# Transposing by halves of 64 rows in a gated-linear-attention and mixer kernel, and copying the first transposes out in two pieces

## The chip, the cores and the metric

The kernel runs on one core of one Trainium2 chip. The metric is device time in microseconds (us) of one execution. Three runs of the kernel before gave 180.56, 180.7 and 180.9 us; the median is 180.7.

## The reference

Two parts follow one another. The first is a recurrent attention with a decaying state, for 4 batches, 8 heads, 768 steps and 48 numbers a head:

```python
for t in range(S):
    state = alpha[:, :, t, :, None] * state + np.einsum('bhd,bhe->bhde', k[:, :, t], v[:, :, t])
    y[:, :, t] = np.einsum('bhd,bhde->bhe', q[:, :, t], state)
```

Its result, laid out as 4 x 768 x 384, goes through a mixer with a residual:

```python
xt = x.transpose(0, 2, 1)
h = np.maximum(xt @ w_tok1, 0.0) @ w_tok2          # 768 -> 256 -> 768, along the steps
u = x + h.transpose(0, 2, 1)
h2 = np.maximum(u @ w_ch1, 0.0) @ w_ch2            # 384 -> 1536 -> 384, along the channels
return (u + h2).astype(np.float32)
```

## The kernel before, in words

**Attention.** Each batch has 6 chunks of 128 steps. ScalarE takes the logarithm of alpha (`la`, L360), TensorE sums it along the chunk with a triangular matrix (`cum`, L461, or L531 and L533), ScalarE makes the exponentials of that sum (`ek` L373, `eq` L375), and GpSimd or VectorE multiplies keys and queries by them (`pkk`, `pkq`, L392). Both products lie with steps on the 128 partitions. TensorE transposes them (L409 or L557): the data is the loaded operand, an identity is the one that streams, and the result lies in a bank of PSUM. ScalarE or VectorE copies that to SBUF (`tk`, `tq`, L413 or L563). From the transposes TensorE makes the scores within a chunk (`gt`, L477 or L574), VectorE masks them (`gm`, L418), and TensorE multiplies them by the values (`y`, L510 or L607), to which it adds the earlier chunks' share (`between`, L447). The state goes through L498 or L595 on TensorE, then `st` and `ss` (L428, L431, L435). The result `x` is copied out at L442.

**Two forms of a chunk.** In batches 0 and 1 (`PLAN` has P there) chunks come in pairs, `paired_chunks`: row p of the two halves of a load holds steps 2p and 2p+1, and rows 0 to 63 belong to the one chunk, 64 to 127 to the other. Some of its matmuls therefore use 64 rows and run in two row halves in turn (L595, L607), or in 64x64 quarters (L574). A pair has 16 transposes, 8 of keys and 8 of queries, in two banks. Batches 2 and 3 (N) use `natural_chunk`: 8 transposes a chunk, 4 and 4, in two banks; its L477 uses 48 of 64 rows in two halves in turn.

**Mixer.** `mixer(b)` has `tok1` (L655, for batch 0 in parts at L635), `tok2` (L674), the residual `u` (L682, L685), the transposes of `u` (L698, 18 of 128x128 a batch) and their copies `ut` (L704), `ch1` (L723, 72 matmuls a batch), its relu `rt` (L642, L644), `ch2` (L738, 72 matmuls a batch) and the sum and the store of the output (L747, L749). In batch 0 the copies of `ut` come in two halves of 3 chunks, in batches 1 to 3 as one piece of 768 columns for each of the 3 blocks of channels.

**Order.** No engine's order is written by hand. Every step is an `Op` in a `Graph`, with a cost for each engine that may run it and a priority that places batch b+1's attention ahead of batch b's `ch1` and `ch2`. `run` simulates the engines: whenever one is free it takes the ready step of best priority, if enough of the 8 banks of PSUM are free. Up to 32 us of that simulation an idle TensorE gets a dummy matmul (L795, 78 in all). `search` tries 600 random changes of the priorities and engines of batch 0, by the simulated end of its `ut` copies. The order found is then emitted, and on the chip every engine works through its own list in order, waiting where an operand is late. A changed cost can so move any step of any engine. Within the simulation a step that writes a bank waits for all earlier readers of that bank.

Of the kernel before, what the change touches and what calls it, by code (L numbers as in the profile page):

```python
# [200 lines left out]
def kernel(  # L201
# [83 lines left out]
    tk_t = many("tk", NG, [128, 4, 128])  # L285
    tq_t = many("tq", NG, [128, 4, 128])
# [7 lines left out]
    ut_t = many("ut", 2 * NM, [128, S])  # L294
# [106 lines left out]
    def s_transpose(n, w, dst, key, prio):  # L401

        u, bank = units[n], Bank()
        src, ksrc = u["p" + w]

        def emit(e):
            ps = banks[bank.place].bitcast(BF16)
            for j in range(4):
                pe.transpose(ps[:, 128 * j : 128 * j + 128], src[:, 2 * j : 2 * j + 2, :], id128)  # L409

        g.add("tr" + w, {"PE": 0.225}, emit, [ksrc], [bank], prio, new=[bank])
        g.add("tp" + w, {"ACT": 0.52, "DVE": 0.40},
              lambda e: evict[e](dst, banks[bank.place].bitcast(BF16)[:, 0:512].rearrange("p (j t) -> p j t", j=4)),  # L413
              [bank], [key], prio)
# [36 lines left out]
    def natural_chunk(n):  # L451
# [17 lines left out]
        tk, tq, i = tk_t[n % NG], tq_t[n % NG], n % NG  # L469
        s_transpose(n, "k", tk, ("tk", i), pr + 2)  # L470
        s_transpose(n, "q", tq, ("tq", i), pr + 2)
        gb = [Bank(), Bank()]

        def gt(e):
            for j in range(4):
                for par in range(2):
                    pe.matmul(banks[gb[par].place][:, 128 * j : 128 * j + 128],  # L477
                              lhsT=tk[64 * par : 64 * par + D, j, :],
                              rhs=tq[64 * par : 64 * par + D, j, :], start=True, stop=True,
                              skip_group_check=True)  # L480

        g.add("gt", {"PE": 0.24}, gt, [("tk", i), ("tq", i)], gb, pr + 1, new=gb)
# [24 lines left out]
        def y(e):  # L507
# [4 lines left out]
            if ci:  # L512
                between(ps, tq, n)

        g.add("y", {"PE": 0.37 if ci else 0.21}, y, [("gm", 2 * i), ("gm", 2 * i + 1), kvb, ("tq", i)] + ([kprev] if ci else []),
# [3 lines left out]
    def paired_chunks(b, sc):  # L519
# [28 lines left out]
        ktk, ktq = ("tk2", i2), [("tq2", i2)]  # L548
        for w in "kq":
            bank = Bank()  # L550
            for s in range(2):
                src, ksrc = us[s]["p" + w]

                def emit(e, w=w, s=s, src=src, bank=bank):
                    ps = banks[bank.place].bitcast(BF16)
                    for j in range(4):
# [277 lines left out]
```

## Time and profile before

| | |
|---|---|
| median of 3 runs | 180.7 us |
| the profiled execution | 180.38 us |
| its span, first to last instruction | 178.7 us |
| TensorE matmuls, busy | 172.5 us, 97% |
| ScalarE, VectorE, GpSimd busy | 100.8, 96.4, 69.1 us |
| granted clock of TensorE | 1.00 |

Time outside the span is 1.68 us. The busy time of TensorE is a sum over intervals whose ends are modelled and which overlap: the pace of a stream of matmuls is read from the starts of successive rows of the timeline, not from the length of one. In a timeline row the first number is the start, the second the length of the whole row, then come engine, line, operation, output and inputs, loaded shape (rows x columns), result shape, and the number of instructions; a bracket gives idle time ahead of the row and what ended it.

### The profile page before, as it was taken

The numbers are of one execution on the slowest core, as the hardware profiler recorded it, in microseconds if no ns is written. First come the engines' busy times: TensorE is split into PE (matmuls) and PEld (weight loads), VectorE is DVE, ScalarE is ACT, GpSimd is POOL, SyncE is SP. The second block draws the span as 40 slices with busy tenths as digits, with TensorE's granted clock in tenths as the row PEclk, the third lists the DMA queues.
The fourth block names the chain that finished last, engine by engine and source line by source line (L and its number), as shares of the span: only waits on it lengthen the run. The fifth ranks groups of instructions, "written<-read, shape, count | busy, mean of one in ns | idle before, by whom it ended". The sixth has DMA issues, their size and how long they took to land.

```text
span 178.7 us, 4775 instructions
## 1 busy us (share of the span) xinstructions
PE 172.5 (97%) x1929; PEld 112.4 (63%) x1929; DVE 96.4 (54%) x197; ACT 100.8 (56%) x206; POOL 69.1 (39%) x111
## 2 busy tenths in 40 slices
PE   6999999999999998999999999999999999999991
PEld 2667666666666766677666566676766666565650
DVE  3269895602277967698982632499754362000321
ACT  2586384699765455678776330598872230996000
POOL 7341580000878975929951111398850000000000
PEclk9999999999999999999999999999999999999999
DMA  5999999999999898989999999700000112100222
GB/s 138 261 261 260 237 283 206 203 218 257 271 265 276 191 233 151 247 154 195 158 202 148 205 193 253 219 0 4 0 4 32 55 45 91 44 0 4 88 88 88
DMA packets 81797, 27.83 MB, mean 156 GB/s; under 512 B 75376, under 2 KB 81520, under 8 KB 81776
## 3 DMA queue, kind: packets, MB, share of 16 engines
q1 hardware_dynamic: 79424, 25.17, 65.7%
q0 software_dynamic: 2352, 2.36, 8.3%
q8 instruction: 15, 0.25, 0.6%
q14 instruction: 6, 0.05, 0.1%
HBM read 25.17 MB, written 4.72 MB: 167 GB/s over the span
## 4 chain that ended last, share of the span: by engine, by line
PE 85%; POOL 7%; issue 3%; DVE 2%; POOLq 0%; DVEq 0%
PE bank L723 26%; PE bank L738 21%; PE bank L795 8%; PE bank L674 4%; PE bank L655 3%; PE bank L409 3%; PE bank L698 2%; PE bank L557 2%; POOL pkq L392 2%; PE bank L477 2%; POOL ss L431 2%; POOL pkk L392 2%; PE bank L447 2%; PE bank L510 1%; PE bank L461 1%
## 5 line engine op out<-in xcount | busy, mean ns | idle before, releaser
L723 PE MATMUL bank<-ut,wc 128*128 128x384 bf16 x288 | 51.9, 326 | 0.0
L738 PE MATMUL bank<-wc,rt 128*128 128x384 bf16 x288 | 50.3, 326 | 0.0
L642 ACT ACTIVATE rt<-bank 128x384 bf16<-128x384 f32 x73 | 35.6, 492 | 8.3 <-PE bank L723 7.8
L738 PEld LDWEIGHTS <-rt 128*128 128x128 bf16 x288 | 27.3, 98 | 17.0
L392 POOL TENSOR_TENSOR pkk<-ink,ek 128x384 bf16<-128x384 f32 x24 | 23.8, 998 | 33.0 <-ACT ek L373 30.9
L723 PEld LDWEIGHTS <-wc 128*128 128x128 bf16 x288 | 26.6, 98 | 15.3
L747 DVE TENSOR_TENSOR o<-bank,u 128x384 f32<-128x384 f32 x24 | 13.3, 556 | 36.7 <-PE bank L738 36.6
L399 POOL CAST vb<-inv 128x384 bf16<-128x384 f32 x22 | 10.8, 503 | 25.0 <-DMA inv<-in_v_dram 25.0
L373 ACT ACTIVATE ek<-bank 128x384 f32<-128x384 f32 x24 | 11.8, 501 | 14.5 <-PE bank L464 9.9
L795 PE MATMUL bank<-zeros,id 128*128 128x384 bf16 x78 | 17.0, 354 | 1.8 <-DVE la L300 1.8
L644 DVE TENSOR_SCALAR rt<-bank 128x384 bf16<-128x384 f32 x23 | 12.3, 554 | 11.4 <-PE bank L723 11.1
L360 ACT ACTIVATE la<-ina 128x384 bf16<-128x384 f32 x24 | 12.1, 529 | 10.6 <-DMA ina<-in_alpha_dram 10.5
L392 POOL TENSOR_TENSOR pkq<-inq,eq 128x384 bf16<-128x384 f32 x18 | 18.0, 998 | 0.0
L418 DVE TENSOR_TENSOR gm<-bank,u 128x512 bf16<-128x512 f32 x24 | 15.4, 683 | 1.2 <-PE bank L477 1.2
L418 DVE TENSOR_TENSOR gm<-bank,pmask 128x512 bf16<-128x512 f32 x24 | 15.0, 683 | 1.4 <-PE bank L574 1.0
L685 DVE TENSOR_TENSOR u<-bank,x 128x384 bf16<-128x384 f32 x21 | 10.3, 550 | 5.7 <-PE bank L674 5.7
L795 PEld LDWEIGHTS <-id 128*128 128x128 bf16 x78 | 7.7, 105 | 6.9 <-POOL id masks.py:199 1.8
L431 POOL TENSOR_TENSOR ss<-st,al 128x384 bf16<-128x384 f32 x12 | 9.9, 827 | 4.0 <-DVE st L428 4.0
L442 ACT CAST x<-bank 128x384 bf16<-128x384 f32 x15 | 7.3, 487 | 5.8 <-PE bank L447 3.6
L375 ACT ACTIVATE eq<-bank 128x388 f32<-128x388 f32 (+2 forms) x18 | 9.2, 511 | 0.0
L674 PE MATMUL bank<-ht,wt 128*128 128x384 bf16 x48 | 8.9, 326 | 0.0
L704 ACT COPY ut<-bank 128x768 bf16<-128x768 bf16 (+1 forms) x8 | 5.5, 722 | 5.8 <-PE bank L698 5.8
(95 smaller groups left out, 209.0 us busy)
## 6 DMA issues: line engine op xcount, KB each, us to landing
out_dram<-o SPq DMA_DIRECT2D x24, 192.0 KB, 2.6
ina<-in_alpha_dram SPq DMA_DIRECT2D x6, 384.0 KB, 6.1
ink<-in_k_dram SPq DMA_DIRECT2D x6, 384.0 KB, 6.2
inq<-in_q_dram SPq DMA_DIRECT2D x6, 384.0 KB, 6.5
inv<-in_v_dram SPq DMA_DIRECT2D x6, 384.0 KB, 6.5
ina<-in_alpha_dram SPq DMA_DIRECT2D x12, 192.0 KB, 4.6
ink<-in_k_dram SPq DMA_DIRECT2D x12, 192.0 KB, 4.6
inq<-in_q_dram SPq DMA_DIRECT2D x12, 192.0 KB, 4.5
```

What stands on the lines that cost most here:

```text
L360: g.add("la", {"ACT": 0.43}, lambda e: act.activation(la[:, :, 0:D], t, AF.Ln), key, [u["la"][1]], pr + 5)
L373: g.add("ek", {"ACT": 0.40}, lambda e: act.activation(ek, banks[bank.place][:, 0:HD], AF.Exp, scale=-1.0), [bank], [kek], pr + 4)
L392: lambda e, dst=dst, src=src, ex=ex: {"POOL": gps, "DVE": dve}[e].tensor_tensor(dst[:, :, 0:D], src, ex().rearrange("p (h d) -> p h d", h= ...
L418: g.add("gm", {"DVE": 0.62}, lambda e: dve.tensor_tensor(gm, banks[bank.place].rearrange("p (j t) -> p j t", j=4), wide(mask, [[0, 4], lis ...
L431: g.add("ss", {"POOL": 0.97}, lambda e: gps.tensor_tensor(ss, st.rearrange("p (h d) -> p h d", h=H), wide(al, [[1, 8], [0, D]]), ALU.mult) ...
L642: act.activation(dst, src, AF.Relu)
L644: dve.tensor_scalar_max(dst, src, 0.0)
L674: pe.matmul(banks[bank.place][:, 0:HD], lhsT=wt2[:, m, i * 128 : i * 128 + 128], rhs=ht_t[b % 2 * NDT + m], start=(m == 0 and not on_act), ...
L723: pe.matmul(banks[bank.place][:, 0:HD], lhsT=wc1[wp][:, kc, off : off + 128], rhs=ut_t[(b % 2) * NM + kc][:, cs], start=(kc == 0), stop=(k ...
L738: pe.matmul(banks[bank.place][:, 0:HD], lhsT=rt_t[(b * NDC + mc) % NRT][:, i * 128 : i * 128 + 128], rhs=wc2[:, mc, :], start=(mc == 0), s ...
L747: g.add("o", {"DVE": 0.49}, lambda e, i=i, bank=bank, o=o: dve.tensor_tensor(o, banks[bank.place][:, 0:HD], u_t[(n0 + i) % NX], ALU.add), ...
L795: return Op("fill", {"PE": 0.33 if now < COLD else 0.17}, lambda e: pe.matmul(banks[N_BANKS - 1][:, 0:HD], lhsT=id128, rhs=zeros, start=Tr ...
```

## The change

Batches 1 to 3 no longer transpose a 128x128 block with one matmul. Rows 0 to 63 and rows 64 to 127 are transposed by two matmuls that follow each other, each with 64 rows loaded and 64 columns streaming, and each half goes to a bank of its own. This holds for keys and queries of `paired_chunks` when b is not 0, for `natural_chunk`, and for the transposes of `u`. A chunk's keys and queries then share the two banks, and the copies take a half each. `ut` becomes one tile for all channel blocks and is made in two groups of 3 chunks in every batch; `ch1` of one half of the columns waits for its own group.

In batch 0 the transposes stay whole; keys and queries of a pair are copied out by two copies of 512 columns each where one of 1024 stood, and the scores of one half of the keys wait only for their part. Some costs that the planner uses are changed with it (`gt`, `state`, `y`).

```diff
+    def row_tiles(place, srcs):
+        for i, src in enumerate(srcs):
+            for h in range(2):
+                rows = slice(64 * h, 64 * h + 64)
+                pe.transpose(banks[place[h].place].bitcast(BF16)[:, 64 * i : 64 * i + 64], src[rows], id128[rows, rows])
+
-    def s_transpose(n, w, dst, key, prio):
-        u, bank = units[n], Bank()
...
-        g.add("tr" + w, {"PE": 0.225}, emit, [ksrc], [bank], prio, new=[bank])
-        g.add("tp" + w, {"ACT": 0.52, "DVE": 0.40},
...
+    def s_transpose(n, dst, key, prio):
+        u, tb = units[n], [Bank(), Bank()]
+        srcs = [u["p" + w][0][:, 2 * j : 2 * j + 2, :] for w in "kq" for j in range(4)]
+        g.add("tr", {"PE": 0.28}, lambda e: row_tiles(tb, srcs), [u["pk"][1], u["pq"][1]], tb, prio, new=tb)
+        for h in range(2):
+            g.add("tp", {"ACT": 0.52, "DVE": 0.40}, lambda e, h=h: evict[e](
+                dst.rearrange("p w j t -> p (w j) t")[:, :, 64 * h : 64 * h + 64],
+                banks[tb[h].place].bitcast(BF16)[:, 0:512].rearrange("p (x t) -> p x t", t=64)),
+                [tb[h]], [(*key, h)], prio)
...
-        g.add("gt", {"PE": 0.24}, gt, [("tk", i), ("tq", i)], gb, pr + 1, new=gb)
+        g.add("gt", {"PE": 0.28}, gt, ktkq, gb, pr + 1, new=gb)
...
+        if b == 0:
+            for w in "kq":
+                bank = Bank()
...
+                for part in range(2):
+                    def evicted(e, w=w, bank=bank, part=part):
...
+                    g.add("tp" + w, {"ACT": 0.52, "DVE": 0.40} if w == "k" else {"ACT": 0.52, "DVE": 0.65}, evicted,
+                          [bank], [(ktk if w == "k" else ktq)[part]], pr + 2)
+        else:
+            tb = [Bank(), Bank()]
+            for w in "kq":
+                for s in range(2):
+                    src, ksrc = us[s]["p" + w]
+                    def emit(e, w=w, s=s, src=src):
+                        at = 512 * (w == "q") + 256 * s
+                        for j in range(4):
+                            for c in range(2):
+                                rows = slice(64 * c, 64 * c + 64)
+                                pe.transpose(banks[tb[c].place].bitcast(BF16)[:, at + 64 * j : at + 64 * j + 64],
+                                             src[rows, 2 * j : 2 * j + 2, :], id128[rows, rows])
+                    g.add("tr" + w, {"PE": 0.14}, emit, [ksrc], tb, pr + 2, new=tb if (w, s) == ("k", 0) else [])
+                for c in range(2):
...
+                    g.add("tp" + w, {"ACT": 0.52, "DVE": 0.40} if w == "k" else {"ACT": 0.52, "DVE": 0.65}, evicted,
+                          [tb[c]], [(ktk if w == "k" else ktq)[c]], pr + 2)
...
-            g.add("gt", {"PE": 0.24}, gt, [ktk, *ktq], gb, pr + 1, new=gb)
+            g.add("gt", {"PE": 0.26}, gt, [ktk[s], *ktq] if b == 0 else [*ktk, *ktq], gb, pr + 1, new=gb)
...
-        g.add("state", {"PE": 0.34 if last else 0.4}, kv, [us[0]["pk"][1], us[1]["pk"][1], *kvb], sbk, pr + 1, new=sbk)
+        g.add("state", {"PE": 0.34 if last else 0.44}, kv, [us[0]["pk"][1], us[1]["pk"][1], *kvb], sbk, pr + 1, new=sbk)
...
-        g.add("y", {"PE": 0.9}, within, [*kgm, *kvb], yb, pr + 1, new=yb)
+        g.add("y", {"PE": 0.52}, within, [*kgm, *kvb], yb, pr + 1, new=yb)
...
-        parts = 2 if b == 0 else 1
-        per = NCH // parts
-        for part in range(parts):
+        ut, per = ut_t[b % 2], NCH // 2
+        for part in range(2):
...
+            if b:
+                tb = [Bank(), Bank()]
+                srcs = [u_t[(n0 + i) % NX][:, j * 128 : j * 128 + 128] for j in range(NM) for i in mine]
+                g.add("utp", {"PE": 0.31}, lambda e, tb=tb, srcs=srcs: row_tiles(tb, srcs), ku, tb, 1000 * b + 170, new=tb)
+                for h in range(2):
+                    g.add("ut", {"ACT": 0.60, "DVE": 0.43}, lambda e, tb=tb, h=h, cs=cs: evict[e](
...
+                continue
```

More of the change, by code (lines that the diff above doesn't have):

```diff
@@ L293 @@
     u_t = many("u", NX, [128, HD])
-    ut_t = many("ut", 2 * NM, [128, S])
+    ut_t = many("ut", 2, [128, NM, S])
     NRT = 2 * NDC
@@ L547, in paired_chunks @@
         tq2, tk2 = tq2_t[i2], tk2_t[i2]
[L548 to L556, printed above, removed]
[L557 to L565 removed]
+        ktk = [("tk2", i2, c) for c in range(2)]
```

83 lines of the change are left out of this document (46 added, 37 removed).

## The prediction

> **What bounds the kernel now.** I read the page first (span, busy shares, chain), then the busy time by stage, then TensorE's timeline, whose starts give every price below.
>
> ```profile
> span 178.7 us, 4775 instructions
> PE 172.5 (97%) x1929; PEld 112.4 (63%) x1929; DVE 96.4 (54%) x197; ACT 100.8 (56%) x206; POOL 69.1 (39%) x111
> ...
> PE 85%; POOL 7%; issue 3%; DVE 2%; POOLq 0%; DVEq 0%
> ```
>
> TensorE is 97% busy and 85% of the chain. The stages, cut at the first `ch1` of batch 0, at that of batch 1 and at the last output sum:
>
> ```profile
> 34.31:79.10 44.79, 44.11 (x605) 29.75 (x603) 25.89 (x48) 30.85 (x63) 26.11 (x38) 1.00 1.08 226
> 79.10:175.10 96.00, 95.93 (x869) 61.47 (x865) 47.90 (x92) 50.54 (x108) 29.26 (x44) 1.00 0.50 99
> ```
>
> The columns are length, then busy us of TensorE, its weight loads, VectorE, ScalarE and GpSimd, then the granted clock (1.00). After 79.10 TensorE never waits; before that it idles visibly for 0.68 us. So the time moves by what TensorE's own list gets longer or shorter, and by its waits around 70 to 79 us. The profiled execution took 180.38 us, 0.32 below the median of 180.7; what the sum gives against it I add to the median.
>
> **Prices.** The pace is the difference between the starts of successive rows.
>
> ```profile
> 21.02 0.57 PE L607 MATMUL bank<-vb,gm 64*128 64x48 bf16 x32
> 21.52 0.34 PE L447 MATMUL bank<-ss,tq 128*128 128x96 bf16 x4
> ...
> 84.09 1.14 PE L723 MATMUL bank<-ut,wc 128*128 128x384 bf16 x6
> 85.16 0.40 PE L477 MATMUL bank<-tq,tk 48*128 48x128 bf16 x8
> 85.49 0.34 PE L461 MATMUL bank<-la,u 128*128 128x384 bf16 x1
> ...
> 86.47 1.14 PE L723 MATMUL bank<-ut,wc 128*128 128x384 bf16 x6
> 87.45 0.36 PE L510 MATMUL bank<-vb,gm 128*128 128x48 bf16 x8
> 87.65 0.33 PE L447 MATMUL bank<-ss,tq 128*128 128x96 bf16 x4
> 87.82 0.39 PE L409 MATMUL bank<-id,pkq 128*128 128x128 bf16 x4
> ...
> 102.64 1.17 PE L698 MATMUL bank<-id,u 128*128 128x128 bf16 x18
> 103.64 0.65 PE L738 MATMUL bank<-wc,rt 128*128 128x384 bf16 x3
> ```
>
> A whole transpose: 18 in 1.00 us, 55.8 ns each. Full-array matmuls of fewer columns: L447, 96 columns, 0.17 us for 4, 42.5 ns; L510, 48 columns, 0.20 us for 8, 25 ns. Entering 64-row work: 6 `ch1` take 1.07 us ahead of L477 but 0.98 ahead of L510, 0.09 more. Inside and leaving it: 8 of L477 (4 pairs of row halves) take 0.33 us; 16 of them, at 75.60 below, take 0.55, so 4 pairs are 0.22, that is 55 ns a pair, as one whole matmul of 128 columns, and 0.11 is fixed. L607's 16 pairs of 48 columns, (0.50 - 0.11)/16, give 24.4 ns, again one whole matmul's 25. So two row halves overlap fully, a pair costs what one matmul of its columns costs, and a change of shape costs about 0.10 us, 0.20 there and back. [...]
>
> **The change, part by part.**
>
> 1. *Transposes.* Whole ones replaced: 48 in batch 1, 96 in batches 2 and 3, 18 for `u` in each of three batches: 198, which become 198 pairs of 64 columns. No row has 64 columns in halves. Bounds: 25 ns (48 columns) and 42.5 (96); I take 29, on the line from 42.5 at 96 to 55.8 at 128, nearest in kind. 198 x (55.8 - 29) = -5.3 us. [...]
>
> 2. *Shape changes.* In the order of the instructions TensorE changes shape 57 times before and 106 times after (19 and 22 of them before the first `ch1`): isolated groups of 8 or 16 halves stand between `ch1` and `ch2`. 49 x 0.10 = +4.9 us, all on TensorE's path. A group of 4 transposes alone (0.22 us) becomes 4 x 0.029 + 0.20 = 0.32: dearer; a chunk's keys and queries together, 0.45 to 0.43; 9 of `u`, 0.50 to 0.46. Work on TensorE: -0.4 us, with bounds of -1.2 (25 ns) and +2.3 (42.5).
>
> 3. *Copies.* Each row ends with busy us and mean ns of one.
>
> ```profile
> L563 ACT COPY tk<-bank 128x1024 bf16<-128x1024 bf16 x4 | 4.0, 1007 | 5.1 <-PE bank L557 5.1
> L413 ACT COPY tk<-bank 128x512 bf16<-128x512 bf16 x8 | 4.8, 597 | 3.1 <-DVE u L685 1.7 <-PE bank L409 1.4
> ```
>
> A pair's 2 copies become 4: 2 x 0.60 for 1.01 on ScalarE, 0.2 us more each time. Natural chunks keep two; `ut` has 4 of 576 where it had 3 of 768. ScalarE is busy 30.85 of 44.79 us in the second stage and VectorE 25.89, so this is covered; where its cover ends is point 5. SP's list has the same loads, with a few output stores moved; GpSimd's has the same multiplies, and one weight cast ahead of two weight loads, 1 us of delay for weights that `ch1` reads some 15 us later: nothing.
>
> 4. *Batch 0.* Its copies in two pieces let scores start earlier, but both orders hold 78 dummy matmuls ahead of `ch1`, so TensorE's list there is as long, plus 3 shape changes (counted above). Its waits may differ by 0.3 us either way; I take 0.
>
> 5. *The end of batch 1's attention.* Here nothing covers TensorE.
>
> ```profile
> 64.96 0.64 PE L574 MATMUL bank<-tq,tk 48*64 48x128 bf16 x32
> 65.53 2.77 PE L738 MATMUL bank<-wc,rt 128*128 128x384 bf16 x16
> 68.15 0.33 PE L461 MATMUL bank<-la,u 128*128 128x384 bf16 x1
> ...
> 69.25 0.51 PE L447 MATMUL bank<-ss,tq 128*128 128x96 bf16 x8
> 70.27 0.34 PE L498 MATMUL bank<-vb,pkk 128*128 128x96 bf16 x4 [0.50 <-POOL pkk L392]
> ...
> 75.60 0.62 PE L477 MATMUL bank<-tq,tk 48*128 48x128 bf16 x16
> 76.15 0.51 PE L498 MATMUL bank<-vb,pkk 128*128 128x96 bf16 x8
> 76.56 0.38 PE L409 MATMUL bank<-id,pkk 128*128 128x128 bf16 x4
> 77.02 1.43 PE L698 MATMUL bank<-id,u 128*128 128x128 bf16 x18
> 78.28 0.36 PE L510 MATMUL bank<-vb,gm 128*128 128x48 bf16 x8
> ```
>
> ```profile
> 65.64 2.47 DVE L418 TENSOR_TENSOR gm<-bank,pmask 128x512 bf16<-128x512 f32 x4
> 74.09 2.87 DVE L685 TENSOR_TENSOR u<-bank,x 128x384 bf16<-128x384 f32 x6
> ```
>
> ```profile
> 68.64 0.49 ACT L373 ACTIVATE ek<-bank 128x384 f32<-128x384 f32 x1 [3.42 <-DVE o L747]
> 69.02 0.49 ACT L375 ACTIVATE eq<-bank 128x388 f32<-128x388 f32 x1
> 70.50 0.57 ACT L360 ACTIVATE la<-ina 128x384 bf16<-128x384 f32 x1
> ```
>
> Before, the last pair's scores (L574) start at 64.96 and their four masks end at 68.11, 3.15 us later; 16 `ch2` cover that. TensorE's waits here are 69.59 to 70.27 (8 x 0.0425 after 69.25), 0.24 ahead of 77.02, 0.26 within the 18 transposes of `u` (1.26 for 1.00) and some 0.1 elsewhere: 1.3 us.
>
> After, the last `ch2` of batch 0 stand ahead of those scores. Behind them come 8 `state`, two `cum` with their totals, 4 `state` and then `y`: 0.57 + 0.44 + 0.53 + 0.17 = 1.7 us of work in the 3.15 that the masks take, so about 1.45 us of waiting. A second wait stands at the same place: ScalarE's list has `ek` and `eq` of batch 2's first chunk ahead of the second chunk's `la`, and TensorE's second `cum` needs that `la`. From the first `cum`: 0.49 to `ek`, 0.38 to `eq`, 0.38 to `la`, 0.52 for it, against 0.26 of own work: 1.5 us. The two run together; I count 1.5. Behind them queue, on TensorE, `state`, `y`, the new transposes, `gt` and `tok1`. Then: the state's chain (sum on VectorE behind the masks, `ss` on GpSimd behind `pkq`) holds the next L449 for 0.3 us; `gt` waits 0.3 for its copies, behind ScalarE's exponentials and an `x`; the second group of `u` transposes stands earlier in the list than the 18 did, and `u` takes 2.87/6 a piece, 0.5. `tok2` finds `ht` ready. Sum 2.6 to 2.7 against 1.3: +1.4 us. Bounds: -0.3, if `cum` and masks come as early as before and only L698's pacing goes, and +2.2, if the two 1.5 us follow each other in part.
>
> 6. *Batches 2 and 3 after that.* 72 `ch1` and 72 `ch2` lie between chunks; the stage had 0.07 us of idle, so only points 1 and 2 count there.
>
> Sum: -5.3 + 4.9 + 1.4 = +1.0 us. The profiled execution becomes 181.4, the median 181.7.
>
> **Rivals.**
>
> *Faster: the gap does not grow.* The price is point 5: it decides when added waiting is under 0.05 us. For it: GpSimd idles 2.57 us before 69.20 already (the row below), so attention is not short of that engine; against it, the program's order has no `ch2` left to fill with.
>
> ```profile
> 69.20 1.00 POOL L392 TENSOR_TENSOR pkk<-ink,ek 128x384 bf16<-128x384 f32 x1 [2.57 <-ACT ek L373]
> ```
>
> Then -0.4 remains: 180.3; with pairs at 25 ns, 179.5. Chance 0.22.
>
> *No change: a pair of 64 columns costs the 25 ns of 48.* Then -6.1 + 4.9 + 1.4 = +0.2: 180.9. For it, 48 columns at 24.4 to 25 look like a floor; against it, 96 and 128 columns lie on a line that meets 25 at 54. [...] Chance 0.14.
>
> *The halves do not overlap.* No transposes in row halves are in the trace, and if each takes its own 29 ns, a pair costs 58: 198 x 29 = 5.7 us more, 187.4. Against it: L477, L595 and L607 all overlap. Chance 0.08.
>
> **How the numbers follow.** My forecast, slower by 0.4 to 2.3 us (181.1 to 183.0), has 0.56. A change of under 0.2%, 0.36 us, can't be told from none. Slower: 0.56 + 0.08 = 0.64; same 0.14; faster 0.22. The range 179.6 to 183.2 takes in the faster case down to 25 ns, and point 5's upper bound with pairs at 31 ns; it leaves out the serial halves and the tails, under 0.2.
>
> **What would show it.** Steps 1 and 2: in the timeline, 18 halves of `u` from start to next start in 0.37 us when alone, 16 halves in 0.34. Step 4: first `ch1` at 34.6. Step 5: idle of about 1.5 us between batch 1's last scores and its `y`, `tok1` of batch 1 near 73 instead of 70.67, first `ch1` of batch 1 near 80.6 instead of 79.10, and 0.4 us less from there to the end. The forecast fails if the pace of a pair is far from 29, or if that gap is covered.

## The result

Four runs of the changed kernel gave 185.48 to 185.86 us, median 185.61; four of the kernel before, 180.56 to 181.32, median 180.8. The ratio is 1.026, with a 95% interval of 1.024 to 1.029. The forecast was 181.7 us, with a range up to 183.2: the sign is right, the size is not, and the time lies above the range.

The page of the changed kernel, its span and busy times, and the first line of its chain:

```profile
span 183.8 us, 5209 instructions
...
PE 175.8 (96%) x2127; PEld 109.4 (60%) x2127; DVE 97.6 (53%) x204; ACT 100.5 (55%) x214; POOL 69.2 (38%) x111
...
PE 94%; ACT 2%; DVE 2%; issue 1%; DVEq 0%; ACTq 0%
```

The profiled execution took 185.5 us. Its span is 5.1 us longer than before's 178.7. Here is the busy time by stage, cut at the same marks as before (first `ch1` of batch 0, that of batch 1, last `ch2`); the columns are those explained in the prediction:

```profile
0.00:36.30 36.30, 33.88 (x463) 21.50 (x464) 21.66 (x61) 19.35 (x40) 14.03 (x30) 1.00 1.08 229
36.30:84.75 48.45, 46.54 (x696) 29.46 (x693) 26.91 (x51) 31.02 (x68) 26.43 (x38) 0.93 1.02 211
84.75:180.20 95.45, 95.41 (x977) 58.44 (x972) 48.45 (x94) 50.16 (x108) 28.70 (x43) 1.00 0.45 95
```

The first stage took 36.3 us where it took 34.3, the middle one 48.45 where it took 44.79, and the last 95.41 where it took 95.95 (both to the last matmul's end). That is +2.0, +3.66 and -0.54, together +5.1. One thing in the second row was not in the forecast at all: a mean granted clock of 0.93. TensorE's timeline shows the place:

```profile
69.28 0.64 PE L611 MATMUL bank<-tq,tk 48*64 48x128 bf16 x32
69.86 0.51 PE L632 MATMUL bank<-vb,pkk 64*128 64x96 bf16 x8
70.30 0.34 PE L463 MATMUL bank<-la,u 128*128 128x384 bf16 x1
70.47 0.24 PE L466 MATMUL bank<-ones_col,la 128*128 128x1 bf16 x4
72.15 0.48 PE L463 MATMUL bank<-la,u 128*128 128x384 bf16 x1 [1.43 <-ACT la L359]
72.42 0.29 PE L466 MATMUL bank<-ones_col,la 128*128 128x1 bf16 x4
72.58 0.48 PE L501 MATMUL bank<-vb,pkk 128*128 128x96 bf16 x4
72.99 0.82 PE L644 MATMUL bank<-vb,gm 64*128 64x48 bf16 x32
...
76.03 3.50 PE L692 MATMUL bank<-x,wt 128*128 128x384 bf16 x12
```

The wait that step 5 foretold is there: the totals that start at 70.47 have begun their last at 70.55, the second `cum` starts at 72.15, 1.6 us later, released by `la`. But 12 matmuls of `tok1` take 3.34 us from the first start to that of the next row at 79.37, 0.28 each, where 6 `ch1` of the same shape took 0.98 before, 0.16 each. Windows of 3.41 us (why these borders, below) show the granted clock, third column from the right:

```profile
65.22:68.64 3.42, 3.42 (x71) 2.28 (x70) 2.61 (x6) 2.14 (x4) 2.57 (x6) 1.00 0.94 205
68.64:72.05 3.41, 2.08 (x50) 1.38 (x49) 2.82 (x6) 1.24 (x3) 0.71 (x2) 1.00 0.80 169
72.05:75.46 3.41, 3.07 (x65) 2.23 (x64) 1.40 (x4) 2.01 (x6) 3.41 (x6) 0.50 1.07 198
75.46:78.88 3.42, 3.39 (x17) 1.70 (x18) 2.09 (x4) 0.78 (x2) 1.34 (x3) 0.50 0.77 136
78.88:82.29 3.41, 3.41 (x49) 2.25 (x47) 2.33 (x5) 2.50 (x6) 1.35 (x3) 1.00 1.25 208
```

From 72.05 to 78.88 TensorE ran at half clock, and only there.

### The profile page after: what moved, and what is told of

The parts are those of the page before. It is cut to its first block, busy times and chain, and to the rows that moved or that the text cites. A ratio compares the mean times of both kernels' runs of the same rounds, so it can differ in the third digit from the quotient of the medians.

```text
span 183.8 us, 5209 instructions
## 1 busy us (share of the span) xinstructions
PE 175.8 (96%) x2127; PEld 109.4 (60%) x2127; DVE 97.6 (53%) x204; ACT 100.5 (55%) x214; POOL 69.2 (38%) x111
## 3 DMA queue, kind: packets, MB, share of 16 engines
q0 software_dynamic: 2352, 2.36, 8.1%
## 4 chain that ended last, share of the span: by engine, by line
PE 94%; ACT 2%; DVE 2%; issue 1%; DVEq 0%; ACTq 0%
PE bank L768 26%; PE bank L783 26%; PE bank L840 8%; PE bank L711 4%; PE bank L692 4%; PE bank L405 3%; PE bank L480 2%; PE bank L449 2%; PE bank L611 2%; PE bank L644 2%; PE bank L632 1%; PE bank L513 1%; PE bank L534 1%; PE bank L562 1%; PE bank L587 1%; PE bank L463 1%
## 5 line engine op out<-in xcount | busy, mean ns | idle before, releaser
L679 ACT ACTIVATE rt<-bank 128x384 bf16<-128x384 f32 x74 | 36.3, 493 | 10.7 <-PE bank L768 10.5
L768 PEld LDWEIGHTS <-wc 128*128 128x128 bf16 x288 | 26.1, 98 | 16.1
L840 PE MATMUL bank<-zeros,id 128*128 128x384 bf16 x78 | 18.1, 365 | 1.8 <-DVE la L299 1.8
L398 POOL CAST vb<-inv 128x384 bf16<-128x384 f32 x21 | 10.3, 504 | 19.9 <-DMA inv<-in_v_dram 16.6
L444 ACT CAST x<-bank 128x384 bf16<-128x384 f32 x14 | 6.7, 481 | 9.3 <-PE bank L449 9.3
L413 ACT COPY tkq<-bank 128x512 bf16<-128x512 bf16 x16 | 9.1, 601 | 1.0 <-PE bank L405 0.9
L735 ACT COPY ut<-bank 128x576 bf16<-128x576 bf16 x7 | 4.4, 642 | 9.0 <-PE bank L405 9.0
```

Of the source, the lines that this page charges most:

```text
L398: lambda e: evict[e](vb, src), ksrc, [u["vb"][1]], pr + 4)
L679: act.activation(dst, src, AF.Relu)
L768: pe.matmul(banks[bank.place][:, 0:HD], lhsT=wc1[wp][:, kc, off : off + 128], rhs=ut_t[b % 2][:, kc, cs], start=(kc == 0), stop=(kc == NM ...
L840: return Op("fill", {"PE": 0.33 if now < COLD else 0.17}, lambda e: pe.matmul(banks[N_BANKS - 1][:, 0:HD], lhsT=id128, rhs=zeros, start=Tr ...
```

## The changed kernel again: three times, not one

It ran ten times more on another occasion, unaltered, and later three times more. The expectations quoted from here on name their theories by letters of their own; the text around them uses words.

> The changed kernel once more, unaltered, in more runs. With whole transposes in the same order a wait of the same 1.6 us did not lower the clock in the profiled run, and its runs lie at 182.2 to 183.0 and at 184.4 to 184.7 us. Theory A2: whether the clock falls after that wait differs from run to run, so the runs lie in two groups some 2 to 2.6 us apart, about 183.2 and 185.6. Theory B2: 64-row work in the same stretch decides it, so every run lies near 185.6.

Its times do not lie about one value. Sorted by the mean granted clock of the execution, all 17 runs:

| mean granted clock | runs | times, us | mean |
|---|---|---|---|
| 0.999 to 1.00 | 4 | 182.58 to 182.99 | 182.75 |
| 0.991 | 7 | 183.39 to 183.87 | 183.63 |
| 0.981 | 6 | 185.48 to 185.86 | 185.66 |

All four runs of the first result belong to the last row. The profiled execution of this second occasion took 183.64 us and had the half clock for 3.42 us instead of 6.83. Without this occasion's two runs of the last row, its ratio to the kernel before is 1.010 (1.006 to 1.013). Against the kernel before in the same job (21 runs, median 181.67), the four undisturbed runs are 1.1 us slower, near the +1.0 of the forecast; by the means, runs with a half clock of 3.4 us take 0.9 more than those, runs with one of 6.8 take 2.9 more.

The kernel before is not quite steady either: a second profiled execution took 183.07 us.

> The kernel before, unaltered, for a second profile: how far the start moves by itself. In the first profile the first sum on TensorE began at 5.90 us, in the five profiles of other kernels at 6.37 to 6.56. If that is the phase of the clock's rise, it lies anywhere from 5.9 to 6.6 here too, and the stretches after the first ch1 repeat to 0.1 us (44.79 and 95.95).

In that execution a load came late: ScalarE's `la` waited for it 3.72 us, the copies of `tk` stood behind it, and TensorE waited 1.29 us in the middle of `u`'s transposes. The two rows of its timeline:

```profile
76.92 1.09 PE L698 MATMUL bank<-id,u 128*128 128x128 bf16 x12
79.30 0.50 PE L698 MATMUL bank<-id,u 128*128 128x128 bf16 x6 [1.29 <-ACT tk L413]
```

So comparisons below use the stages of a profile for sizes and the ratios of several runs for verdicts.

## Experiments on the end of batch 1's attention

**The wait filled.** Nine dummy matmuls stand where TensorE waits for `la`; nothing else is changed.

```diff
         def cum(e):
             ps = banks[bank.place]
+            for _ in range(9 if (b, ci) == (2, 1) else 0):
+                pe.matmul(ps[:, 0:HD], lhsT=id128, rhs=zeros, start=True, stop=True, skip_group_check=True)
```

> The changed kernel with its own order, and 9 dummy matmuls of 384 columns (1.46 us) put ahead of the second sum of batch 2, where TensorE waited 1.6 us. Theory A: the wait itself let TensorE's clock fall to half from 72 to 79 us, which cost about 2.6 us; with the wait filled the granted clock stays 1.00, tok1 of batch 1 takes 1.95 us and not 3.34, the stretch from the first ch1 to batch 1's first ch1 is 45.8 us and not 48.45, the time is about 183.0 us. Rival B: the clock fell because of the 64-row work, not for the wait: half clock stays, 185.6 us. Rival C: the clock costs nothing that is not waited for anyway: clock 1.00, but still over 185 us.

Ten runs: 182.16 to 183.87 us, ratio 1.0097 (1.0066 to 1.0128), and a mean clock of at least 0.997 in every one. Its timeline in place of the rows above:

```profile
70.70 0.24 PE L468 MATMUL bank<-ones_col,la 128*128 128x1 bf16 x4
70.83 1.62 PE L464 MATMUL bank<-zeros,id 128*128 128x384 bf16 x9
72.38 0.32 PE L465 MATMUL bank<-la,u 128*128 128x384 bf16 x1
```

The second `cum` starts no earlier in relation to the first, so the dummies shorten nothing on the path; the middle stage falls from 48.45 to 46.01 us all the same. The half clock was worth these 2.4 us, and with the wait filled none of the ten runs had it, where 13 of the changed kernel's 17 did.

**Whole transposes in the order of the change.** Each pair of halves becomes one 128x128 transpose; order, banks and number of copies stay.

```diff
-            for h in range(2):
-                rows = slice(64 * h, 64 * h + 64)
-                pe.transpose(banks[place[h].place].bitcast(BF16)[:, 64 * i : 64 * i + 64], src[rows], id128[rows, rows])
+            h, x = (i % 2, i // 2) if len(srcs) == 8 else (i // 6, i % 6)
+            pe.transpose(banks[place[h].place].bitcast(BF16)[:, 128 * x : 128 * x + 128], src, id128)
...
-                            for c in range(2):
-                                rows = slice(64 * c, 64 * c + 64)
-                                pe.transpose(banks[tb[c].place].bitcast(BF16)[:, at + 64 * j : at + 64 * j + 64],
-                                             src[rows, 2 * j : 2 * j + 2, :], id128[rows, rows])
+                            pe.transpose(banks[tb[s].place].bitcast(BF16)[:, at + 128 * j : at + 128 * j + 128],
+                                         src[:, 2 * j : 2 * j + 2, :], id128)
```

The copies read and write accordingly.

> The changed kernel with its own order, banks and copies, but every pair of 64-row transposes is one whole 128x128 transpose, so that those shape changes and the overlap are gone. Theory A (the halves are worth 0.4 to 0.5 us in all, and the wait at batch 1's end drops the clock): the wait is still there, the clock falls as well, about 186.0 us, 0.5 slower than the changed kernel. Rival B (64-row work drops the clock): clock 1.00, about 182.6 us. Rival D (the shape changes cost more than was worked out): without a gap in the clock's favour it is faster than the changed kernel by over 1 us.

Four runs: 182.24 to 184.71 us, ratio 1.011 (1.004 to 1.018); two had a mean clock of 0.987, the profiled one did not. The wait is still 1.60 us:

```profile
69.84 0.24 PE L465 MATMUL bank<-ones_col,la 128*128 128x1 bf16 x4
71.52 0.32 PE L462 MATMUL bank<-la,u 128*128 128x384 bf16 x1 [1.43 <-ACT la L359]
```

So the order makes the wait, and the halves do not. The middle stage is 46.05 us against 46.01 with halves (both without half clock), and the last one 95.75 against 95.41: the halves by themselves are worth 0.33 us, all in batches 2 and 3.

**Both together**, the dummies and the whole transposes by the two diffs above.

> Both edits together: whole transposes in the changed kernel's order, and the 9 dummy matmuls. Against the run with the dummies alone it measures what the halves are worth at full clock. Theory A: 0.4 to 0.5 us slower than that one, about 183.4. Rival D: faster than that one by over 0.5 us.

Six runs: 182.31 to 183.63 us, ratio 1.008 (1.005 to 1.012); middle stage 46.04, last 95.75. By the stages it adds up as the two edits one by one. The medians do not show the halves' 0.33 us, 182.86 here against 183.1 with the dummies alone: runs of one kernel lie further apart than that. The rival, faster by over 0.5 us, is not borne out.

**When the clock falls.** The moment at which the clock rises at the start differs from run to run. The granted clock column shows 1.00 there from the beginning, so it is read from the steps of equal matmuls of 384 columns. After the change:

```profile
6.55 0.53 PE L534 MATMUL bank<-la,u 128*128 128x384 bf16 x1
6.88 0.49 PE L536 MATMUL bank<-la,u 128*128 128x384 bf16 x1
7.20 0.33 PE L534 MATMUL bank<-la,u 128*128 128x384 bf16 x1
7.36 0.33 PE L536 MATMUL bank<-la,u64s 128*128 128x384 bf16 x1
```

Steps of 0.33 and 0.32 us up to 7.20, of 0.16 after it. From 7.20 to the fall at 72.05 are 64.85 us, 19.00 times 3.413; half of the 6.83 us at half clock is 3.415. In the second profile of the changed kernel the clock rose at 5.29 and fell at 73.55, 68.26 us or 20.00 times 3.413 later, to rise again at 76.97, 3.42 us after the fall. So in both profiles the fall and the rise behind it lie, to 0.02 us, on borders 3.413 us apart that are counted from the rise at the start; the stretch between two borders is called a window here. A wait of 1.6 us sufficed for a fall where most of it lay in one window (TensorE busy for 2.08 of its 3.41 us).

Three more profiled executions of the changed kernel tested the borders, together with a version that has two dummies in the place of nine (`range(2 ...)` in the diff above).

> The changed kernel unaltered; one look. Theory W: the clock is decided by windows of 3.413 us that run on from the moment at which it rose at the start (after: 7.20 us, drop from 72.05 to 78.88 us, 19 and 21 windows later; changed_again: 5.29, from 73.55 to 76.97, 20 and 21 later; pieces_from_own_banks: 4.93, from 73.17 to 76.58, 20 and 21 later), and a window in which TensorE was busy for less than about 2.3 of its 3.41 us is followed by one at half clock. Then from this profile: the rise at the start gives the borders; if one window around 70 to 73 us shows TensorE busy for under 2.25 us, the clock is 0.50 from that window's end for 3.41 or 6.83 us; if the wait of 1.6 us is cut by a border so that both windows keep over 2.35 us, there is no drop. Rival R: where the borders lie decides nothing; then a drop begins off the borders, or a window under 2.25 us goes without one.

> The changed kernel unaltered, a second look for the same question, since the borders lie elsewhere in each run: by theory W the drop, if any, begins a whole number of windows of 3.413 us after the rise at the start (to 0.1 us) and follows a window with TensorE busy for under 2.25 us; a run whose windows all keep over 2.35 us shows none. By the rival R the drop keeps to no border.

> The changed kernel unaltered, a third look for the same question. Theory W: as for the two before, drop only behind a window with TensorE busy for under 2.25 us, and from that window's end. Rival R: no such tie.

> The changed kernel with two dummies (instead of nine) where batch 2's second cum stands, right behind the wait: they cannot start earlier than the wait of their bank lets them, and take up 0.33 us of the 1.6. By theory W the worst window, 2.06 to 2.08 us busy without them, has 2.39 to 2.41 with them wherever the borders lie, which is over the 2.36 us of the emptiest window so far that was not followed by a drop: no run with a mean clock of 0.99 or 0.98, and 182.4 to 183.3 us. Rival: the length of the wait decides, which is still 1.27 us and as long as the one ahead of the drop in pieces_from_own_banks: then runs of 183.7 and 185.6 us come in as in the changed kernel.

All three executions of the changed kernel had the half clock, for one window, at the border counted from their own start (rises at 4.98, 5.28 and 4.94 us; falls at 73.25, 73.55 and 73.21). Windows of the first of the three (the third profile of this kernel), with the borders worked out from its start:

```profile
69.84:73.25 3.41, 1.89 (x65) 1.60 (x64) 2.28 (x5) 2.79 (x7) 2.94 (x5) 1.00 0.92 204
73.25:76.66 3.41, 3.33 (x21) 1.61 (x19) 2.28 (x5) 1.15 (x3) 2.48 (x4) 0.50 0.88 162
76.66:80.07 3.41, 3.41 (x49) 2.31 (x48) 2.30 (x6) 2.34 (x6) 1.19 (x2) 1.00 1.23 209
```

And of the kernel with whole transposes, where the border at 71.14 cut the same wait of 1.60 us in two and the clock did not fall:

```profile
67.73:71.14 3.41, 2.36 (x52) 1.57 (x50) 2.91 (x6) 1.26 (x4) 0.82 (x2) 1.00 0.92 211
71.14:74.56 3.42, 2.86 (x67) 2.17 (x67) 1.98 (x5) 2.79 (x7) 3.42 (x5) 1.00 1.11 196
```

In the table, "work" is a sum made for this comparison: a matmul of 384 columns with 128x128 loaded counts 0.16 us, the step measured above, and one with fewer columns, or with less loaded (rows x columns), is counted in proportion.

| profiled execution | emptiest window near the wait | TensorE busy in it, us of 3.41 | work in it, us | clock in the next |
|---|---|---|---|---|
| changed, fifth | 69.79 to 73.21 | 1.90 | 1.16 | 0.50 |
| changed, third | 69.84 to 73.25 | 1.89 | 1.15 | 0.50 |
| changed, again | 70.14 to 73.55 | 2.05 | 1.18 | 0.50 |
| changed, fourth | 70.13 to 73.55 | 2.05 | 1.18 | 0.50 |
| changed, first | 68.64 to 72.05 | 2.08 | 1.18 | 0.50 |
| pieces from own banks (below) | 69.78 to 73.20 | 2.23 | 1.25 | 0.50 |
| whole transposes | 67.73 to 71.14 | 2.36 | 1.46 | 1.00 |
| batch 0 as before (below) | 71.06 to 74.47 | 2.39 | 1.42 | 1.00 |
| scores beside transposes (below) | 68.00 to 71.41 | 2.48 | 1.44 | 1.00 |
| two dummies | 69.31 to 72.72 | 2.35 | 1.34 | 1.00 |
| before, second profile | 76.30 to 79.71 | 1.99 | 1.39 | 1.00 |

The place was right three times in three. The expectation of the two-dummy kernel was not: 4 of its 12 runs had a mean clock of 0.991 (the ratio over all is 1.008, 1.005 to 1.011, times 181.78 to 184.04). Its premise, that no window there can hold less than 2.39 us, does not hold in its own trace. The first row is where the borders lay in the profiled execution, whose clock rose at 4.45; the second is a stretch 0.29 us later, where another run's border may fall:

```profile
69.31:72.72 3.41, 2.35 (x68) 1.74 (x67) 2.33 (x5) 2.44 (x6) 2.50 (x3) 1.00 0.98 217
69.60:73.01 3.41, 2.08 (x63) 1.56 (x62) 2.28 (x5) 2.73 (x7) 2.79 (x4) 1.00 0.95 210
```

What busy time does not explain is the last row of the table, with its wait in the middle of `u`'s transposes: full clock behind 1.99. Work, counted so, does sort it. In all 17 profiles, some 860 windows counted forward and back from each rise, the 24 with work of up to 1.25 us were followed by half clock and all others, from 1.32 us on, by full clock; 17 of the 24 lie ahead of the rise at the start. This was found in the traces afterwards, and no run was made to test it. With 1.28 us as the level (an estimate, between these two figures), 85% of all positions of a border give the changed kernel such a window (13 of its 17 runs had the half clock), 25% the one with two dummies (4 of 12), none the one with nine (0 of 10); 73% give it to the scores beside transposes, where only 3 of 10 runs had it, so the fit of the shares is loose. What the profiles themselves show is that all six falls began 19 or 20 times 3.413 us after the rise, and that in three kernels where a border cut the wait (whole transposes at 71.14 us, batch 0 as before at 71.06, scores beside transposes at 71.41) the clock stayed at 1.00.

## Experiments on batch 0

**Batch 0's copies in one piece again**, the rest as changed; newly planned, 82 dummies.

```diff
-                for part in range(2):
-                    def evicted(e, w=w, bank=bank, part=part):
...
-                    g.add("tp" + w, {"ACT": 0.52, "DVE": 0.40} if w == "k" else {"ACT": 0.52, "DVE": 0.65}, evicted,
-                          [bank], [(ktk if w == "k" else ktq)[part]], pr + 2)
+                g.add("tp" + w, {"ACT": 0.95, "DVE": 0.62} if w == "k" else {"ACT": 0.97, "DVE": 1.17},
+                      lambda e, dst=dst, bank=bank, form=form: evict[e](
+                          dst, banks[bank.place].bitcast(BF16).rearrange(form, **({"s": 2} if "s" in form else {}))),
+                      [bank], ktk if w == "k" else ktq, pr + 2)
```

> The changed kernel, but batch 0's keys and queries are copied out by one copy of 1024 columns each as before; the planner finds an order of its own for it. Theory E: in the changed kernel the two copies of a bank follow each other on two engines and delay the scores, which made 1.2 of the 2.0 us by which the first ch1 came late; here it comes at 34.3 to 35.0 us, depending on when the clock rises at the start, and the time falls by about 1.2 us, to 184.4, if the wait at batch 1's end stays as long. Rival F: the delay is only the start's clock, and the first ch1 stays near 36.

Runs of 182.34, 182.65, 183.51 and 185.29 us: the three groups again (mean clock 0.999 and 1.00, 0.991, 0.981); ratio 1.012 (1.005 to 1.020) without the last. For batch 0 the first stage is compared without what the half clock at the start cost (each step of 384 columns longer than 0.163 us until the rise): before 34.31 - 1.68 = 32.63; after 36.30 - 2.65 = 33.65, and 33.65 to 33.84 in eight other profiles of the same batch 0. Here it is 35.43 - 2.15 = 33.28 with 4 dummies more, 0.65 us at 0.163 each: 32.6 without them. So the pieces cost 1.0 us.

**Only the pieces, in the kernel before**; newly planned, 76 dummies.

```diff
+            if b == 0:
+                for part in range(2):
...
+                    g.add("tp" + w, {"ACT": 0.52, "DVE": 0.40} if w == "k" else {"ACT": 0.52, "DVE": 0.65}, evicted,
+                          [bank], [(ktk if w == "k" else ktq)[part]], pr + 2)
+                continue
```

> The kernel before, with only batch 0's copies in two pieces (the planner finds an order of its own). Theory E: the second copy of a bank waits for the first, on another engine, and the first ch1 comes 0.7 to 1.5 us later than with one copy each (34.3 in the profile of before, of which up to 0.65 is when the clock rises at the start), so the time is 181.8 to 182.6 us unless the rest of the order moves too. Rival F: the first ch1 stays within 0.3 us once the start's clock is taken off, and the time within 0.5 us of before.

Four runs: 183.37 to 184.18 us, ratio 1.013 (1.009 to 1.017). That is above the 181.8 to 182.6 expected. The first stage is 33.36 us without the start's half clock, and has 2 dummies less than before, so +1.1 again. The middle stage grew to 48.04 us: the planner put another order there, with four waits of 0.4 to 0.7 us by the starts from 70 to 81 us and 32 matmuls of attention that the kernel before has in its last stage, so this kernel tells of batch 0's pieces only in its first stage.

**Where the 1.0 us comes from.** In the changed kernel ScalarE's and VectorE's timelines show the two copies of one bank of queries:

```profile
11.43 0.58 ACT L571 COPY tq<-bank 128x512 bf16<-128x512 bf16 x1 [1.43 <-DVE tq L571]
...
25.32 0.58 ACT L571 COPY tq<-bank 128x512 bf16<-128x512 bf16 x1 [0.60 <-DVE tq L571]
```

```profile
10.65 0.69 DVE L571 COPY tq<-bank 128x512 bf16<-128x512 bf16 x1 [0.74 <-PE bank L562]
...
24.59 0.69 DVE L571 COPY tq<-bank 128x512 bf16<-128x512 bf16 x1 [0.45 <-PE bank L562]
```

VectorE's piece ends at 11.34, ScalarE's begins at 11.43; at 25.28 and 25.32 likewise. Two engines were given half each, and took turns. TensorE waits for the second piece twice:

```profile
12.07 0.32 PE L534 MATMUL bank<-la,u 128*128 128x384 bf16 x1 [0.18 <-ACT tq L571]
...
25.95 0.42 PE L611 MATMUL bank<-tq,tk 48*64 48x128 bf16 x16 [0.42 <-ACT tq L571]
```

By the starts these are 0.32 and 0.59 us, together 0.9. To test it, each piece was given a bank of its own:

```diff
-                bank = Bank()
+                two = [Bank(), Bank()]
...
-                            pe.transpose(ps[:, 512 * s + 128 * j :][:, 0:128], src[:, 2 * j : 2 * j + 2, :], id128)
+                            ps = banks[two[s if w == "k" else j // 2].place].bitcast(BF16)
+                            at = 128 * j if w == "k" else 512 * s + 128 * (j % 2)
+                            pe.transpose(ps[:, at : at + 128], src[:, 2 * j : 2 * j + 2, :], id128)
```

> The changed kernel with batch 0's two pieces each in a bank of its own, so that two engines copy out at once; newly planned, with 80 dummies in the place of 78. If the copies of one bank one after the other are what batch 0 lost, the queries' copies on ScalarE and VectorE overlap, TensorE's two waits in batch 0 (0.32 and 0.59 us) are gone, and the first stretch without the half clock at the start takes 33.65 - 0.9 + 0.33 for two more dummies = 33.1 us, against 33.65 to 33.8 after the change; ratio to before near 1.007. Rival: what batch 0 lost is the order that the pieces bring and their shape changes, or the writing of one tile by two engines; then it stays at 33.6 or more and the ratio is that of the changed kernel.

Its two pieces now run beside each other, on ScalarE and on VectorE:

```profile
10.04 0.57 ACT L573 COPY tq<-bank 128x512 bf16<-128x512 bf16 x1
...
23.22 0.62 ACT L573 COPY tq<-bank 128x512 bf16<-128x512 bf16 x1
```

```profile
9.92 0.68 DVE L573 COPY tq<-bank 128x512 bf16<-128x512 bf16 x1
...
23.22 0.69 DVE L573 COPY tq<-bank 128x512 bf16<-128x512 bf16 x1 [0.44 <-PE bank L564]
```

The first stage is 34.37 - 1.52 = 32.85 us with 80 dummies, 32.5 with 78: the 1.0 us is gone together with the turns and with both waits. The plan is a new one, and it changes shape 19 times ahead of the first `ch1`, as the kernel before, where the changed kernel does 22 times; so part of the gain, 0.3 us at 0.10 a change, may be the order's and not the banks'. The time as a whole is no better, 182.69 to 184.76 us in six runs, ratio 1.012 (1.008 to 1.016) where 1.007 was expected: the new order leaves three waits between 67 and 72 us, and every run had the half clock (0.991 twice, 0.981 four times).

## Experiments on the shape changes, and the version that is faster

**Scores beside transposes.** Batch 0 in one piece, and a chunk's scores (`gt`) are made one step with the next chunk's transposes, so that TensorE enters work of 64 rows once for both.

```diff
+            def together(e):
+                gt(e)
+                row_tiles(tb, srcs)
+
+            g.add("tr", {"PE": 0.66}, together, [u["pk"][1], u["pq"][1], *ktkq], [*tb, *gb], prio, new=[*tb, *gb])
```

> The changed kernel with batch 0's copies as before, and in batches 2 and 3 the scores of a chunk and the transposes of the next chunk as one step, so that they share one visit to 64-row work: 32 shape changes after batch 1's first ch1 instead of 44. Theory A: a change costs 0.10 us, so that stretch falls from 95.43 to about 94.2 us; the stretch before it stays near 46.1; about 181.8 us. Rival D2: changes cost nothing that counts, and the stretch stays within 0.3 of 95.4; or the chunks' longer chain shows up as waits and eats the 1.2.

Ten runs: 181.07 to 182.40 us, ratio 1.0014 (0.9986 to 1.0041); three of them had a mean clock of 0.991. The last stage is 94.95 us against 95.43 before this edit, 0.48 less for 12 shape changes fewer (32 in the place of 44 after batch 1's first `ch1`), where 1.2 less had been expected. But the two stages do not hold the same work. The matmuls of `gt` alone in each, first with this edit, then without:

```profile
81.27:176.22 94.95, 4.37 (x88) 2.48 (x88) 1.00 0.46 99
81.55:176.98 95.43, 3.97 (x80) 2.27 (x80) 1.00 0.45 98
```

Here 8 more of them lie behind the cut, and with them 8 of `y` and 16 halves of transposes: 0.22 + 0.20 + 0.23 = 0.65 us by the prediction's prices. For equal work the stage is thus 1.13 us shorter, an estimate, or 0.09 for each change taken away. That agrees with the price worked out for adding one.

**Halves only in batches 2 and 3**, batches 0 and 1 as before the change; once with scores and transposes apart, once beside each other.

```diff
+        if n < 2 * NCH:
+            for i, w in enumerate("kq"):
...
+                g.add("tr" + w, {"PE": 0.225}, emit, [u["p" + w][1]], [tb[i]], prio, new=[tb[i]])
...
-        if b == 0:
+        if b < 2:
...
+            if b == 1:
+                for j in range(NM if part == 0 else 0):
...
+                    g.add("utp", {"PE": 0.335}, utp, [("u", (n0 + i) % NX) for i in range(NCH)], [bank], 1000 * b + 170, new=[bank])
```

> Batches 0 and 1 as in the kernel before; halves in batches 2 and 3, with the order of the change (scores and transposes apart). If the loss lies in batch 0's pieces and at the end of batch 1's attention, the first stretch is that of before (34.3 us), the middle 44.8 us, and the rest 95.4 us as after the change, against 95.95: 0.5 us less, ratio 0.997. Rival: the halves of batch 2's first chunks lengthen the wait ahead of batch 1's tok1; then the middle stretch takes 46.0 us and the ratio is 1.004.

> Batches 0 and 1 as in the kernel before (whole transposes, copies in one piece, 78 dummies); halves only in batches 2 and 3, and there the scores of a chunk stand beside the next chunk's transposes. If the loss lies in batch 0's pieces and at the end of batch 1's attention, and the gain in batches 2 and 3, then from the start to the first ch1 it takes what the kernel before takes (34.3 us, 32.65 without the half clock at the start), to batch 1's first ch1 44.8 us, and the rest 94.95 us as in the run with the scores beside the transposes, against 95.95: 1.0 us less, ratio 0.994. Rival: the first halves of batch 2 stand ahead of batch 1's tok1, and what lengthens the wait there is they and not batch 1's own transposes; then the middle stretch takes 45.6 us as it did in that run and the ratio is 0.999.

| | first stage without the start's half clock | middle | last | ratio to before |
|---|---|---|---|---|
| before | 32.63 | 44.79 | 95.95 | |
| apart | 32.68 | 45.12 | 95.42 | 0.996 (0.993 to 0.9995) |
| beside each other | 33.15 | 44.41 | 95.09 | 0.989 (0.986 to 0.992) |

The first one gave 180.02 to 182.46 us in eight runs, the second 178.71 to 181.97 in six, median 180.1, against 181.76 for 13 runs of the kernel before in the same job; the second one's ratio leaves out its run of 181.97. The middle stage of the second:

```profile
34.71:79.12 44.41, 43.64 (x621) 29.06 (x619) 25.13 (x47) 31.04 (x63) 27.11 (x39) 1.00 1.09 228
```

The wait of 1.6 us is gone, what is left at its place is the 0.49 us for `pkk` that the kernel before has too, and no run had a mean clock under 0.997:

```profile
70.67 0.34 PE L534 MATMUL bank<-vb,pkk 128*128 128x96 bf16 x4 [0.49 <-POOL pkk L391]
70.85 1.46 PE L720 MATMUL bank<-x,wt 128*128 128x384 bf16 x8
```

By the stages the gain is 0.7 us, by the medians 1.7; that the runs show more than the profile is unexplained (the kernel before was slower in this job than in the first one). Both measures say faster than before the change, by 0.4 to 1%. No run has whole transposes in the order of the second one, so how much of its gain belongs to that order and how much to the halves is not shown.

## Why the prediction was right or wrong

**Step 1, a pair at 29 ns: right.** With 16 halves alone (4 pairs of keys, 4 of queries) the step to the next work is 0.34 us, as forecast, and 18 of `u` take 0.36 to 0.37:

```profile
89.39 0.29 PE L405 MATMUL bank<-id,pkk 64*128 64x64 bf16 x8
89.52 0.28 PE L405 MATMUL bank<-id,pkq 64*128 64x64 bf16 x8
89.73 1.64 PE L768 MATMUL bank<-ut,wc 128*128 128x384 bf16 x9
```

The 0.34 holds 8 x 0.029 and about 0.10 of shape change. The halves do overlap: in the trace successive pairs start 29 ns apart, the two halves of a pair 2 to 4 ns. The rival by which they do not is out, and so is the one with 25 ns. The 29 was read off a line through whole matmuls of 96 and 128 columns, and it held.

**Step 2, 0.10 us a shape change: right.** The last stage, where only steps 1 and 2 count, fell by 0.54 (forecast 0.4). In the order of the change the halves bring it 24 shape changes more and make 108 of its transposes 0.0268 us shorter each, 2.9 in all; it got 0.33 shorter, which leaves 0.11 for a change. Taken away again by joining, 12 changes were worth 0.09 each, for equal work.

**Step 3, copies covered: right** for batches 1 to 3: ScalarE is busy for 31.02 of 48.45 us in the middle stage (30.85 of 44.79 before), and TensorE idles for 0.04 us in the last one. One wait of 0.27 us for copies shows at 75.49, which step 5 had counted with 0.3.

**Step 4, batch 0's waits at 0: wrong.** It allowed for 0.3 us either way. Without the start's half clock the first stage is 1.0 us longer; of that, 0.3 are the three shape changes counted in step 2, at 0.10 each, and 0.9 are two waits for second pieces; the 0.2 by which these are too much is not traced. The step saw that dummies and instructions are as many and left out that the two copies of one bank do not run side by side. Another 0.97 us of the profiled difference (2.65 against 1.68 us) is the moment at which the clock rises (7.20 us after the change, 5.2 before), and no work of the change.

**Step 5, +1.4 us at the end of batch 1's attention: right in mechanism and place, and short of what follows from it.** ScalarE's timeline has the list that was named, `ek`, `eq`, `la`, from the first `cum` on:

```profile
70.81 0.49 ACT L372 ACTIVATE ek<-bank 128x384 f32<-128x384 f32 x1 [2.19 <-PE bank L466]
71.20 0.49 ACT L374 ACTIVATE eq<-bank 128x388 f32<-128x388 f32 x1
71.57 0.53 ACT L359 ACTIVATE la<-ina 128x384 bf16<-128x384 f32 x1
```

and VectorE's masks end at 72.34, so the two waits run together, as counted:

```profile
69.87 2.47 DVE L420 TENSOR_TENSOR gm<-bank,pmask 128x512 bf16<-128x512 f32 x4
```

Without the half clock the middle stage is 46.0 us, which is the 80.6 - 34.6 of the forecast. The step failed in that its wait was priced by its own length alone: a window with TensorE busy for 2.08 of 3.41 us was followed by half clock, which cost 2.4 us more in the execution first profiled, 1.5 in the next, and nothing in 4 runs of 17. (Between runs it shows as 2.9 and 0.9, and part of that is the start: the clock rose there at 7.20 us in the first of these executions and at 5.29 in the second, which cost 2.65 and 1.72 us.) In the trace of before the granted clock was 1.00 in every stage, so nothing in it priced this.

**Step 6: right**, see step 2.

**The rivals.** "The gap does not grow" was wrong: it grew from 0.70 to 1.60 us. What brought the miss is none of the four cases: a half clock behind a wait. Sum by measured terms: +1.0 in batch 0, +1.2 at the wait, +2.4 for the half clock, +1.0 for the clock's later rise, -0.5 in batches 2 and 3, together the 5.1 us of the profiled difference. Without the half clock and with equal starts it is +1.7 by the profiles; the undisturbed runs gave +1.1, and the forecast +1.0. That these two agree is in part luck: the forecast holds nothing for the 0.7 us by which batch 0 came out longer than its three shape changes, and why the runs show 0.6 less than the profiles stays open.

## What to carry to other kernels

Price a new wait of TensorE by more than its length: the half clock behind one of 1.6 us cost 2.4 us more in one execution of the changed kernel, 1.5 in another, and nothing in 4 runs of 17. In the profiles of this case a window with up to 1.25 us of work, summed as above, was followed by half clock and one with 1.32 or more was not, which was found afterwards and not tested. Where the borders lie differed from run to run (rises from 4.4 to 7.7 us). Where work is to be had, even dummies, fill the wait: nine dummies kept the clock up in all of 10 runs, two did not in 4 of 12. When a copy is cut in two for two engines, see in the timeline that the two pieces overlap: here two out of one bank took turns (VectorE's ended at 11.34 us, ScalarE's began at 11.43) and the pieces cost 1.0 us, and two out of a bank each ran together (9.92 and 10.04). And where one edit both helps and harms, measure stage by stage: here halves paid only in batches 2 and 3, and the version that keeps them there alone is faster than both kernels.

## What was not expected of the hardware

- The granted clock fell to 0.50 behind waits of 1.6 us and less (TensorE busy for 1.89 to 2.23 of 3.41 us), for 3.41 or 6.83 us, and each of the six falls seen in a profile began 19 or 20 times 3.413 us after the clock's rise at the start. In 17 profiles the windows with up to 1.25 us of work, as summed above, had half clock behind them, those with 1.32 us and more full clock; ahead of the rise at the start, a window with 1.24 us was followed by none and one with 1.35 us by the rise.
- That rise came between 4.4 and 7.7 us after the start of the span, from run to run; each 384-column matmul ahead of it took 0.32 us instead of 0.163, so it alone moved the first stage by up to 1.6 us (1.30 to 2.87 us of loss in 17 profiles).
- Two copies of 512 columns out of one bank, by two engines, ran one after the other (11.34 to 11.43, 25.28 to 25.32); out of two banks they ran together (9.92 and 10.04, 23.22 and 23.22). The bracket names a semaphore of VectorE, so the program orders them; whether the chip would run both out of one bank was not tried.
